# Converting float64 weights at two of every three second products instead of at each

## The chip, the cores and the metric

The kernel runs on one core of a Trainium2 chip. The metric is the device time of one execution in microseconds (us); of several executions the median counts. The core has five engines that each work through their own instruction list in order: TensorE (PE, with its weight loads shown apart as PEld), VectorE (DVE), ScalarE (ACT), GpSimd (POOL) and SyncE (SP), which here only issues transfers.

## The reference

Retention attention over 1152 tokens gives `x` (1152 x 512). Then comes a mixture of four experts, each `relu(x @ w1[e]) @ w2[e]`, weighted by probabilities and summed, and then one more block with other weights:

```python
def _moe2_ref(x, w_in, w_out):          # x (1152, 512), w_in (512, 2048), w_out (2048, 512)
    h = x @ w_in
    sp = np.where(h > 20.0, h, np.log1p(np.exp(np.minimum(h, 20.0))))
    g = h * np.tanh(sp)                 # mish
    return (g @ w_out).astype(np.float32)
```

`w_in` and `w_out` are float32 arrays multiplied by a float64 scalar and reach the kernel as float64, 8 bytes a value; the kernel makes float32r parts of them by taking their bits apart.

## The kernel before, in words

**Precision.** Every operand of a large matmul is held as two float32r parts, `hi` and `lo` (index 0 and 1 of a tile's second axis), and every product is three matmuls (hi·lo, hi·hi, lo·hi).

**Stages.** The attention stage fills the first 57 us or so. Then the two feed-forward blocks run as 144 *steps*, in the order that the list `seq` of `tile_order` gives; this text numbers them 0 to 143. A step is `("w1", u, c, tb)` or `("w2", u, c, tb)`: `u` is a slice of 512 hidden features (0 to 7 are the experts, 8 to 11 the last block), `c` one of two chunks of 256 output features, `tb` one of three blocks of 384 tokens. Each step is 24 matmuls of 128x128 weights by 128x384 into a tile `ps` of a PSUM pool with four buffers.

- A w1 step (`m1`; `first`, line 403) is followed by `relu_out`: ACT copies with Relu (L424), DVE takes the remainder (L425). From u = 8 on it is `mish_out`: ACT L433, ACT L434, DVE L435.
- A w2 step (`m2`; `second`, line 416) is followed on DVE by L463 (times the probabilities, out of PSUM) and L464 (add to `acc`); at u = 7 also by ACT L469 and POOL L470, which make the two parts of the next block's input `x2`. At u = 8 it is ACT L472, above that DVE L474.
- From step 6 to step 83 the list alternates w2 and w1 steps, in blocks of three token blocks: w2, w1, w2, w1, w2, w1. Such a run of six steps is called a *group* here. Steps 88 to 91 are four w2 steps in a row; step 92 is the first w1 step of the last block, and reads `x2` of token block 0; step 96 is the next that reads a new token block, `x2` of token block 1, which steps 91 and 93 make.

**Weights.** The experts' weights are float32: SP loads a chunk into a tile `wr` (L99), ACT makes `hi` (L114), POOL makes `lo` (L115). This is `split_w`, which runs once a chunk's buffer is free, in the alternating part twice a group, after the last two steps of the group.

**Float64 weights.** The last block has 16 chunks, each in two *halves*, 32 halves in all. One half goes through: a load by SP (L332, `load64`), `exponents64` (DVE L352, then ACT L356 and L357; DVE L358, L361), `values64` (DVE L371, L375, L378, then ACT L381, and the load of a later half), `rest64` (DVE L389), `store64` (SP L338, into a scratch tensor in device memory). From u = 8 on `split_w` only loads a finished chunk from that scratch tensor (L111). All these tiles and `wr` share one pool, `wraw`, of five buffers.

**What sets the order.** Everything is recorded under a manual schedule: each engine runs its instructions in the order in which the loop at the end of the kernel writes them. The loop takes up the four functions at every w2 step, `store64` and `values64` ahead of `m2`, `rest64` and `exponents64` behind it, so that one half is worked on by `exponents64` at one w2 step and by `values64` and `rest64` at the next. Such a w2 step is called a *turn* below. The 32 halves take the w2 steps 1 to 32 for `exponents64`, steps 6 to 68 of the list; the last store is written at step 72.

Of the kernel before, what the change touches and what calls it, by code (L numbers as in the profile page):

```python
# [59 lines left out]
def f32(ap):  # L60
    return ap.bitcast(F32)
# [3 lines left out]
def retention_moe_mish(ctx: ExitStack, tc: tile.TileContext, q2, k2, kt_in, v, vt_in, probs, w1, w2, w64, cdec, dec, out):  # L65
# [36 lines left out]
    def split_w(lo_engine):  # L102
        i = n_split[0]
        if i >= len(order):
            return
        n_split[0] += 1
        key = order[i]
        w = wsp.tile([P, 2, 4, 256], F32R, tag="w", name="w")
        w_t[key] = w
        if key[1] >= NE:  # L110
            sp.dma_start(out=f32(w), in_=scratch[key])  # L111
            return
        t = raw_t.pop(key)
        act.activation(out=w[:, 0], in_=t, func=AF.Copy)  # L114
        lo_engine.tensor_tensor(out=w[:, 1], in0=t, in1=f32(w[:, 0]), op=ALU.subtract)  # L115
        load_w()
# [207 lines left out]
    def load64():  # L324
        i = n_ld[0]
        if i >= len(halves):
            return
        n_ld[0] += 1
        (m, u, c), half = halves[i]
        t = wraw.tile([P, 2, 256, 2], U32, tag="wr", name="w64")  # L330
        src = w64[0 if m == "w1" else 1, u - NE, c, :, 2 * half:2 * half + 2]
        sp.dma_start(out=t, in_=src.bitcast(U32).rearrange("p k (n t) -> p k n t", t=2))  # L332
        raw64[i] = t

    def store64():
        if stores:
            key, half, t = stores.pop(0)
            sp.dma_start(out=scratch[key][:, :, 2 * half:2 * half + 2], in_=f32(t))  # L338
# [3 lines left out]
    def exponents64():  # L342

        i = n_cv[0]
        if i >= len(halves):
            return
        n_cv[0] += 1
        t = raw64.pop(i)
        lo_w, hi_w = t[:, :, :, 0], t[:, :, :, 1]
        g = ph.tile([P, 2, 256], F32, tag="g", name="g64", bufs=4)  # L350
        e = ph.tile([P, 2, 256], U32, tag="g", name="e64", bufs=4)
        dve.tensor_scalar(  # L352
            out=e, in0=hi_w, scalar1=20, scalar2=0x7FF,
            op0=ALU.logical_shift_right, op1=ALU.bitwise_and,
        )
        act.activation(out=e, in_=e, func=AF.Relu, bias=cbias[:, 0:1])  # L356
        act.activation(out=e, in_=e, func=AF.Relu, bias=cbias[:, 1:2], scale=-1.0)  # L357
        dve.tensor_scalar(  # L358
            out=g.bitcast(U32), in0=hi_w, scalar1=0xFFFFF, scalar2=None, op0=ALU.bitwise_and
        )  # L360
        dve.scalar_tensor_tensor(  # L361
            out=g, in0=lo_w, scalar=2.0 ** -32, in1=g.bitcast(U32), op0=ALU.mult, op1=ALU.add
        )
        flight.append((i, hi_w, g, e))

    def values64():
        if not flight or len(flight[0]) != 4:
            return
        i, hi_w, g, e = flight.pop(0)
        st = wraw.tile([P, 2, 2, 256], F32R, tag="wr", name="st64")  # L370
        dve.tensor_scalar(  # L371
            out=e, in0=e, scalar1=23, scalar2=0x7F800000,
            op0=ALU.logical_shift_left, op1=ALU.bitwise_xor,
        )
        dve.scalar_tensor_tensor(  # L375
            out=e, in0=hi_w, scalar=0x80000000, in1=e, op0=ALU.bitwise_and, op1=ALU.bitwise_or
        )
        dve.scalar_tensor_tensor(  # L378
            out=g, in0=g, scalar=2.0 ** 20, in1=e.bitcast(F32), op0=ALU.add, op1=ALU.mult
        )  # L380
        act.activation(out=st[:, 0], in_=g, func=AF.Copy, scale=2.0 ** -20)  # L381
        load64()
        flight.append((i, g, st))

    def rest64():
        if not flight or len(flight[0]) != 3:
            return
        i, g, st = flight.pop(0)
        dve.scalar_tensor_tensor(  # L389
            out=st[:, 1], in0=g, scalar=2.0 ** -20, in1=f32(st[:, 0]),  # L390
            op0=ALU.mult, op1=ALU.subtract,
        )
        stores.append((*halves[i], st))
# [47 lines left out]
    def m1(u, c, tb):  # L441
        o = first(x if u < NE else x2[0], w_t["w1", u, c], tb)
        h_t[u, c, tb] = relu_out(o) if u < NE else mish_out(o)

    def load_pb(e, tb):
        if e < E:
            pb = ph.tile([P, TB], F32, tag=f"pb{tb}", name="pb", bufs=1)
            row = p_dram[e:e + 1].rearrange("e n t -> e (n t)")[:, tb * TB:(tb + 1) * TB]
            sp.dma_start(out=pb, in_=row.to_broadcast([P, TB]))
            pb_t[e, tb] = pb  # L450

    def m2(u, c, tb, js=range(2)):
        ts = slice(tb * TB, (tb + 1) * TB)
        ks = slice(2 * c + js.start, 2 * c + js.stop)
        a = acc[:, ks, ts]
        o = second([h_t[u, i, tb] for i in range(2)], w_t["w2", u, c], js)
        if u < NE:
            pbb = pb_t[u // 2, tb].unsqueeze(1).to_broadcast([P, 2, TB])
            if u == 0:
                dve.tensor_tensor(out=a, in0=o, in1=pbb, op=ALU.mult)  # L460
                return
            t = ph.tile([P, 2, TB], F32, tag="n", name="t", bufs=3)
            dve.tensor_tensor(out=t, in0=o, in1=pbb, op=ALU.mult)  # L463
            dve.tensor_tensor(out=a, in0=a, in1=t, op=ALU.add)  # L464
            if u == NE - 1:
                if x2[0] is None:
                    x2[0] = keep.tile([P, 2, NPAIR, N], F32R, tag="x", name="x2")
                xo = x2[0][:, :, ks, ts]
                act.activation(out=xo[:, 0], in_=a, func=AF.Copy)  # L469
                pool.tensor_tensor(out=xo[:, 1], in0=a, in1=f32(xo[:, 0]), op=ALU.subtract)  # L470
        elif u == NE:
            act.activation(out=a, in_=o, func=AF.Copy)  # L472
        else:
            dve.tensor_tensor(out=a, in0=a, in1=o, op=ALU.add)  # L474
            if u == NU - 1:
                sp.dma_start(out=out[:, ks, ts], in_=a)

    with tc.manual_schedule():
        for tb in range(NTB):
            load_pb(0, tb)  # L480
        for i, (m, u, c, tb) in enumerate(seq):
            if m == "w1":
                m1(u, c, tb)
                if u == 0 and tb + 3 * c < 2:
                    load64()
            else:
                store64()
                values64()
                if i + 1 < len(seq):
                    m2(u, c, tb)  # L490
                else:
                    m2(u, c, tb, range(1))
                    m2(u, c, tb, range(1, 2))
                if u % 2 == 1 and c == 1:
                    load_pb(u // 2 + 1, tb)
                rest64()
                exponents64()
            k = n_split[0]
            if k < len(order) and last_use[order[k - 5]] <= i:
                split_w(pool)  # L500
# [67 lines left out]
```

## Time and profile before

| what | value |
|---|---|
| device time, median of 3 runs | 670.44 us (668.06 to 670.47) |
| the profiled execution | 667.62 us |
| its span on the core | 665.7 us |
| PE busy | 651.3 us, 98% of the span, 3846 matmuls |
| DVE busy | 355.1 us, 53% |
| ACT busy | 216.4 us, 32% |
| POOL busy | 98.1 us, 15% |
| granted TensorE clock, mean | 0.999 |

The span runs from the first to the last instruction; what lies around it is 667.62 − 665.70 = 1.92 us. Busy shares are means over the whole span: DVE's 53% is made of stretches over 80% and of stretches under 20%, so what DVE is worth must be read stretch by stretch. In the timeline a line is a run of instructions of one kind; behind it, in brackets, stands the time in which the engine did nothing before it, and what ended that.

### The profile page before, as it was taken

How to read it: one execution, taken by the hardware profiler on the slowest of the kernel's cores; microseconds unless marked ns; L12 is line 12 of the kernel's file. 1: busy time of each engine (PE TensorE's matmuls, PEld its weight loads, DVE VectorE, ACT ScalarE, POOL GpSimd, SP SyncE). 2: the span in 40 equal slices, each digit the busy share in tenths (PEclk: the TensorE clock that was granted, in tenths of full speed). 3: DMA queues.
4: the chain of work that ended last, by engine and by line, in shares of the span. 5: the costliest groups of instructions: out<-in, count | busy, mean ns of one | idle time of the engine just before them, and what ended most of it. 6: DMA issues, size and time to landing. Idle time of an engine off the chain costs nothing.

```text
span 665.7 us, 9178 instructions
## 1 busy us (share of the span) xinstructions
PE 651.3 (98%) x3846; PEld 646.9 (97%) x3846; DVE 355.1 (53%) x489; ACT 216.4 (32%) x296; POOL 98.1 (15%) x65
## 2 busy tenths in 40 slices
PE   7999999999999999999999999999999999999997
PEld 7999999999999999899898999999999999999997
DVE  4675267788787877888778733243311122222222
ACT  5773234434324344333443221112322211111200
POOL 4320202202022021120220331021100000000000
PEclk9999999999999999999999999999999999999999
DMA  8962224464654644545435311101312330330112
GB/s 295 391 233 82 82 79 142 147 203 128 194 159 130 194 133 145 187 162 193 138 118 189 119 44 51 63 15 48 127 65 77 115 138 1 111 142 1 64 48 95
DMA packets 30498, 83.99 MB, mean 126 GB/s; under 512 B 2994, under 2 KB 8698, under 8 KB 28410
## 3 DMA queue, kind: packets, MB, share of 16 engines
q1 hardware_dynamic: 30458, 83.42, 37.1%
q8 instruction: 30, 0.49, 0.3%
q14 instruction: 10, 0.08, 0.0%
HBM read 64.25 MB, written 19.15 MB: 125 GB/s over the span
## 4 chain that ended last, share of the span: by engine, by line
PE 63%; DVE 18%; ACT 7%; DMA 6%; issue 5%; SPq 1%; ACTq 0%
PE ps L403 28%; PE ps L416 28%; DVE e L375 5%; DMA w<-st 5%; DVE h L425 4%; ACT h L424 3%; PE ps L244 3%; DVE t L463 2%; DVE e L371 2%; ACT e L356 2%; PE ps L208 2%; DVE st L389 2%; ACT w L114 1%; DVE g L378 1%; DVE e L352 1%
## 5 line engine op out<-in xcount | busy, mean ns | idle before, releaser
L403 PE MATMUL ps<-x,w 128*128 128x384 f32 x1728 | 310.8, 335 | 3.4 <-DVE h L425 3.4
L416 PE MATMUL ps<-h,w 128*128 128x384 f32 x1728 | 310.3, 334 | 3.7 <-DVE t L463 3.7
L416 PEld LDWEIGHTS ps<-h,w 128*128 128x128 f32 x1728 | 300.2, 188 | 5.1 <-DVE t L463 5.0
L403 PEld LDWEIGHTS ps<-x,w 128*128 128x128 f32 x1728 | 300.1, 188 | 5.0 <-DVE h L425 5.0
L115 POOL TENSOR_TENSOR w<-wr,w 128x1024 fp32r<-128x1024 f32 x27 | 67.9, 2532 | 299.3 <-ACT w L114 265.3
L425 DVE SCALAR_TENSOR_TENSOR h<-ps,h 128x768 fp32r<-128x768 f32 x48 | 45.9, 957 | 89.8 <-ACT h L424 89.8
L435 DVE TENSOR_TENSOR h<-m,h 128x768 fp32r<-128x768 f32 x24 | 23.1, 960 | 126.2 <-ACT h L434 126.2
L424 ACT ACTIVATE h<-ps 128x768 fp32r<-128x768 f32 x48 | 38.4, 801 | 62.8 <-PE ps L403 57.6
L433 ACT ACTIVATE m<-ps 128x768 f32<-128x768 f32 x24 | 19.6, 815 | 113.5 <-PE ps L403 113.4
L381 ACT ACTIVATE st<-g 128x512 fp32r<-128x512 f32 x32 | 20.2, 633 | 111.2 <-DVE g L378 100.3
L463 DVE TENSOR_TENSOR t<-ps,pb 128x768 f32<-128x768 f32 x42 | 40.0, 952 | 26.7 <-PE ps L416 26.7
L356 ACT ACTIVATE e<-e,cbias 128x512 uint32<-128x512 uint32 x32 | 23.2, 725 | 65.7 <-DVE e L352 65.7
L375 DVE SCALAR_TENSOR_TENSOR e<-w,e 128x512 uint32<-128x512 uint32 x32 | 42.9, 1340 | 1.1
L464 DVE TENSOR_TENSOR acc<-acc,t 128x768 f32<-128x768 f32 x42 | 40.6, 966 | 1.4
L114 ACT ACTIVATE w<-wr 128x1024 fp32r<-128x1024 f32 x32 | 33.6, 1049 | 6.9 <-PE ps L416 6.8
L474 DVE TENSOR_TENSOR acc<-acc,ps 128x768 f32<-128x768 f32 (+1 forms) x19 | 17.3, 912 | 34.6 <-PE ps L416 34.6
L389 DVE SCALAR_TENSOR_TENSOR st<-g,st 128x512 fp32r<-128x512 f32 x32 | 24.1, 753 | 0.0
L357 ACT ACTIVATE e<-e,cbias 128x512 uint32<-128x512 uint32 x32 | 23.2, 724 | 1.0
L361 DVE SCALAR_TENSOR_TENSOR g<-w,g 128x512 f32<-128x512 uint32 x32 | 22.2, 693 | 1.1
L378 DVE SCALAR_TENSOR_TENSOR g<-g,e 128x512 f32<-128x512 f32 x32 | 22.1, 692 | 1.1
L371 DVE TENSOR_SCALAR e<-e 128x512 uint32<-128x512 uint32 x32 | 20.9, 652 | 0.0
L434 ACT ACTIVATE h<-m 128x768 fp32r<-128x768 f32 x24 | 20.4, 848 | 0.8
(46 smaller groups left out, 249.5 us busy)
## 6 DMA issues: line engine op xcount, KB each, us to landing
wr<-w SPq DMA_DIRECT2D x32, 512.0 KB, 4.0
w<-w SPq DMA_DIRECT2D x32, 512.0 KB, 3.9
w<-st SPq DMA_DIRECT2D x32, 512.0 KB, 4.8
w<-w SPq DMA_DIRECT2D x16, 1024.0 KB, 4.8
vr<-v SPq DMA_DIRECT2D x8, 288.0 KB, 5.4
pb<-p_dram SPq DMA_DIRECT2D x12, 192.0 KB, 3.7
kr<-k SPq DMA_DIRECT2D x7, 288.0 KB, 5.3
qr<-q SPq DMA_DIRECT2D x7, 288.0 KB, 6.4
```

Source lines behind the costliest of these rows:

```text
L114: act.activation(out=w[:, 0], in_=t, func=AF.Copy)
L115: lo_engine.tensor_tensor(out=w[:, 1], in0=t, in1=f32(w[:, 0]), op=ALU.subtract)
L356: act.activation(out=e, in_=e, func=AF.Relu, bias=cbias[:, 0:1])
L371: dve.tensor_scalar(out=e, in0=e, scalar1=23, scalar2=0x7F800000, op0=ALU.logical_shift_left, op1=ALU.bitwise_xor,)
L375: dve.scalar_tensor_tensor(out=e, in0=hi_w, scalar=0x80000000, in1=e, op0=ALU.bitwise_and, op1=ALU.bitwise_or)
L389: dve.scalar_tensor_tensor(out=st[:, 1], in0=g, scalar=2.0 ** -20, in1=f32(st[:, 0]), op0=ALU.mult, op1=ALU.subtract,)
L403: pe.matmul(o[:, j, :TB], w[:, a, k, fs], xs[:, c, k, ts], start=k == 0 and n == 0, stop=k == 3 and n == 2,)
L416: pe.matmul(o[:, j, :TB], w[:, a, f, ds_], h[:, c, f % 2], start=f == 0 and n == 0, stop=f == 3 and n == 2,)
L424: act.activation(out=h[:, 0], in_=o, func=AF.Relu)
L425: dve.scalar_tensor_tensor(out=h[:, 1], in0=o, scalar=0.0, in1=f32(h[:, 0]), op0=ALU.max, op1=ALU.subtract)
L463: dve.tensor_tensor(out=t, in0=o, in1=pbb, op=ALU.mult)
L464: dve.tensor_tensor(out=a, in0=a, in1=t, op=ALU.add)
```

## The change

The four conversion functions are no longer called at every w2 step, but only at two of three: a counter `n_y` counts the w2 steps, and where it is a multiple of three the step is written without them. Nothing else differs; the operations, their shapes and their number are the same. In the alternating part the third w2 step of each group, `tb` = 2, is without a turn. The 32 halves now take w2 steps 1 to 47 for `exponents64`: the last is step 97 of the list, and the last store comes at step 102.

```diff
+        n_y = 0
         for i, (m, u, c, tb) in enumerate(seq):
...
             else:
-                store64()
-                values64()
+
+                n_y += 1
+                turn = n_y % 3 != 0
+                if turn:
+                    store64()
+                    values64()
                 if i + 1 < len(seq):
                     m2(u, c, tb)
...
-                rest64()
-                exponents64()
+                if turn:
+                    rest64()
+                    exponents64()
```

Two places show how instructions move. The first is DVE's list in the alternating part (the experts with u = 5). Before, every pair of a w1 and a w2 step reads like this one; `e`, `g`, `w` and `st` are the tiles of a half, `h`, `t` and `acc` those of the steps:

```order
L425 SCALAR_TENSOR_TENSOR h<-ps,h 128x768
L371 TENSOR_SCALAR e_2053<-e_2053 128x512
L375 SCALAR_TENSOR_TENSOR e_2053<-w_1949,e_2053 128x512
L378 SCALAR_TENSOR_TENSOR g_2052<-g_2052,e_2053 128x512
L463 TENSOR_TENSOR t<-ps,pb 128x768
L464 TENSOR_TENSOR acc<-acc,t 128x2x384
L389 SCALAR_TENSOR_TENSOR st_2088<-g_2052,st_2088 128x512
L352 TENSOR_SCALAR e_2125<-w_2021 128x512
L358 TENSOR_SCALAR g_2124<-w_2021 128x512
L361 SCALAR_TENSOR_TENSOR g_2124<-w_2021,g_2124 128x512
```

With the change two pairs of three read as above, and the third is bare; here is the end of a turn, the bare pair and the beginning of the next turn:

```order
L352 TENSOR_SCALAR e_2397<-w_2289 128x512
L358 TENSOR_SCALAR g_2396<-w_2289 128x512
L361 SCALAR_TENSOR_TENSOR g_2396<-w_2289,g_2396 128x512
L425 SCALAR_TENSOR_TENSOR h<-ps,h 128x768
L463 TENSOR_TENSOR t<-ps,pb 128x768
L464 TENSOR_TENSOR acc<-acc,t 128x2x384
L425 SCALAR_TENSOR_TENSOR h<-ps,h 128x768
L371 TENSOR_SCALAR e_2397<-e_2397 128x512
L375 SCALAR_TENSOR_TENSOR e_2397<-w_2289,e_2397 128x512
L378 SCALAR_TENSOR_TENSOR g_2396<-g_2396,e_2397 128x512
```

What moved: the bare pair has three DVE instructions instead of ten, and what followed stands later in the list.

The second place is DVE's list around steps 88 to 93, where the experts end and the last block begins. Before, no conversion is left there; from step 88 on the list reads:

```order
L463 TENSOR_TENSOR t<-ps,pb 128x768
L464 TENSOR_TENSOR acc<-acc,t 128x2x384
L463 TENSOR_TENSOR t<-ps,pb 128x768
L464 TENSOR_TENSOR acc<-acc,t 128x2x384
L463 TENSOR_TENSOR t<-ps,pb 128x768
L464 TENSOR_TENSOR acc<-acc,t 128x2x384
L463 TENSOR_TENSOR t<-ps,pb 128x768
L464 TENSOR_TENSOR acc<-acc,t 128x2x384
L435 TENSOR_TENSOR h<-m,h 128x768
```

With the change turns stand at steps 88, 90 and 91. From the L463 of step 90 on:

```order
L463 TENSOR_TENSOR t<-ps,pb 128x768
L464 TENSOR_TENSOR acc<-acc,t 128x2x384
L389 SCALAR_TENSOR_TENSOR st_3756<-g_3718,st_3756 128x512
L352 TENSOR_SCALAR e_3793<-w_3684 128x512
L358 TENSOR_SCALAR g_3792<-w_3684 128x512
L361 SCALAR_TENSOR_TENSOR g_3792<-w_3684,g_3792 128x512
L371 TENSOR_SCALAR e_3793<-e_3793 128x512
L375 SCALAR_TENSOR_TENSOR e_3793<-w_3684,e_3793 128x512
L378 SCALAR_TENSOR_TENSOR g_3792<-g_3792,e_3793 128x512
L463 TENSOR_TENSOR t<-ps,pb 128x768
L464 TENSOR_TENSOR acc<-acc,t 128x2x384
```

What moved: two consecutive w2 steps (90 and 91) now have a whole half's work between their products.

## Rows read from the trace of the kernel before

**Rows 1.** Part 1 of the page, TensorE: busy time, share of the span, instructions.

```profile
PE 651.3 (98%) x3846; PEld 646.9 (97%) x3846; DVE 355.1 (53%) x489; ACT 216.4 (32%) x296; POOL 98.1 (15%) x65
```

**Rows 2.** Busy time by stretch: length, then each engine, granted clock, DMA share, GB/s.

```profile
250.00:300.00 50.00, 47.45 (x271) 46.49 (x270) 41.42 (x55) 18.32 (x25) 9.90 (x4) 1.00 0.50 166
...
450.00:500.00 50.00, 50.00 (x290) 50.00 (x289) 13.42 (x14) 14.16 (x18) 6.08 (x4) 1.00 0.24 85
```

**Rows 3.** Who TensorE waited for: us in total, times, longest us.

```profile
PE ps L416 <- DVE t L463: 3.7, 4, 0.9
PE ps L403 <- DVE h L425: 3.4, 5, 0.7
```

**Rows 4.** Timeline of TensorE: steps 7, 47, 88 to 91, and 92.

```profile
82.21 4.32 PE L403 MATMUL ps<-x,w 128*128 128x384 f32 x24
...
249.58 4.43 PE L403 MATMUL ps<-x,w 128*128 128x384 f32 x24 [0.68 <-DVE h L425]
...
428.99 16.80 PE L416 MATMUL ps<-h,w 128*128 128x384 f32 x96
...
445.63 4.32 PE L403 MATMUL ps<-x,w 128*128 128x384 f32 x24
```

**Rows 5.** Timeline of DVE: one ordinary pair, from its L371 to the next.

```profile
249.45 0.41 DVE L371 TENSOR_SCALAR e<-e 128x512 uint32<-128x512 uint32 x1
...
251.23 0.95 DVE L463 TENSOR_TENSOR t<-ps,pb 128x768 f32<-128x768 f32 x1
...
252.22 0.96 DVE L464 TENSOR_TENSOR acc<-acc,t 128x768 f32<-128x768 f32 x1
...
253.09 0.69 DVE L389 SCALAR_TENSOR_TENSOR st<-g,st 128x512 fp32r<-128x512 f32 x1
...
256.36 0.96 DVE L425 SCALAR_TENSOR_TENSOR h<-ps,h 128x768 fp32r<-128x768 f32 x1 [1.18 <-ACT h L424]
257.24 0.42 DVE L371 TENSOR_SCALAR e<-e 128x512 uint32<-128x512 uint32 x1
```

**Rows 6.** Timeline of POOL and DVE: the pair in which POOL splits weights.

```profile
264.45 4.95 POOL L115 TENSOR_TENSOR w<-wr,w 128x1024 fp32r<-128x1024 f32 x2 [22.20 <-ACT w L114]
...
265.98 1.16 DVE L371 TENSOR_SCALAR e<-e 128x512 uint32<-128x512 uint32 x1
...
267.17 2.77 DVE L375 SCALAR_TENSOR_TENSOR e<-w,e 128x512 uint32<-128x512 uint32 x1
...
293.12 1.16 DVE L371 TENSOR_SCALAR e<-e 128x512 uint32<-128x512 uint32 x1
```

**Rows 7.** Timeline after the conversion: a bare pair's L463 and L464 beside POOL.

```profile
383.43 0.96 DVE L463 TENSOR_TENSOR t<-ps,pb 128x768 f32<-128x768 f32 x1 [2.36 <-PE ps L416]
...
384.42 0.96 DVE L464 TENSOR_TENSOR acc<-acc,t 128x768 f32<-128x768 f32 x1
384.62 3.02 POOL L115 TENSOR_TENSOR w<-wr,w 128x1024 fp32r<-128x1024 f32 x1 [10.01 <-ACT w L114]
```

**Rows 8.** DMA issues: KB each, median us from issue to landing (half loaded, half stored).

```profile
w<-w SPq DMA_DIRECT2D x32, 512.0 KB, 3.9
w<-st SPq DMA_DIRECT2D x32, 512.0 KB, 4.8
```

**Rows 9.** Timeline of the hand-over: L463 of step 88, table load, x2 of step 93, step 96.

```profile
433.35 0.96 DVE L463 TENSOR_TENSOR t<-ps,pb 128x768 f32<-128x768 f32 x1 [2.35 <-PE ps L416]
...
448.68 1.28 ACT L433 ACT_TABLE_LOAD   x1
...
457.06 1.84 POOL L470 TENSOR_TENSOR x<-acc,x 128x768 fp32r<-128x768 f32 x1 [6.48 <-ACT x L469]
...
462.27 4.32 PE L403 MATMUL ps<-x,w 128*128 128x384 f32 x24
```

**Rows 10.** Groups of instructions on ACT: busy us, mean ns of one, idle before.

```profile
L433 ACT ACTIVATE m<-ps 128x768 f32<-128x768 f32 x24 | 19.6, 815 | 113.5 <-PE ps L403 113.4
...
L356 ACT ACTIVATE e<-e,cbias 128x512 uint32<-128x512 uint32 x32 | 23.2, 725 | 65.7 <-DVE e L352 65.7
```

## The prediction

> **What bounds the kernel now.** The page's first part comes first: TensorE is busy for 98% of the span [rows 1], so only what stops TensorE, or runs before or after it, can be worth anything. Then the busy times by stretch: in 450 to 500 us TensorE is busy all the time and DVE for 13.42 us of 50; in 250 to 300 us TensorE lacks 2.55 us and DVE is busy for 41.42 us [rows 2]. The granted clock is 1.00 in both, so the clock explains nothing. The waits name the engine: TensorE waits nine times for DVE, 3.7 + 3.4 = 7.1 us in all [rows 3], each time for a PSUM buffer that DVE has not read out.
>
> These 7.1 us are not the whole loss, since a stalled step's matmuls are also drawn longer (4.43 us for a step instead of 4.32). The starts tell it better. Steps 88 to 92 start 445.63 − 428.99 = 16.64 us apart over four steps, 4.16 us a step. From step 7 (82.21) to step 88 (428.99) are 81 steps, which at 4.16 would be 336.96 us; they took 346.78 [rows 4]. **The conversion stretch loses 9.82 us.**
>
> Why DVE is late there: an ordinary pair of steps costs it 257.24 − 249.45 = 7.79 us [rows 5], under TensorE's 2 × 4.16 = 8.32. But once a group POOL splits two chunks, and then L371 takes 1.16 us instead of 0.42 and L375 2.77, while the pair of POOL operations lasts [rows 5, 6]. So a group costs DVE 293.12 − 265.98 = 27.14 us [rows 6], against 6 × 4.16 = 24.96 for TensorE. DVE loses 2.18 us a group. For the first groups the four PSUM buffers hide that; the first stall is at step 47 [rows 4].
>
> **The change, part by part.**
>
> *The group.* One pair of three loses its conversion. Of 7.79 us the bare pair keeps L463 until L464 starts (252.22 − 251.23 = 0.99), L464 (253.09 − 252.22 = 0.87) and L425 (257.24 − 256.36 = 0.88), 2.74 in all; 1.18 is idle time before L425, behind ACT's two conversion operations [rows 5]. What is surely gone is 7.79 − 2.74 − 1.18 = 3.87 us. The group becomes at most 27.14 − 3.87 = 23.27 us, 1.69 below TensorE's 24.96. DVE then waits for TensorE once a group and starts each group without a debt; within a group the split pair of 27.14 − 2 × 7.79 = 11.56 us is 3.24 above 8.32, and three other PSUM buffers (12.5 us of TensorE's work) stand between it and a stall. I take the whole 9.82 us. The value is bounded below by what a collision in the bare pair could take back (second rival).
>
> *POOL and ACT.* Without conversion operations ahead of it, ACT makes the first `hi` right at the end of the skipped step, so POOL's first split now runs beside the bare pair. A bare pair beside POOL exists in this trace: L464 at 384.42 takes 0.96 us, and POOL, which starts 0.20 later, takes 3.02 [rows 7]. There POOL waits and DVE does not. So I cost this at nothing; at worst L464 waits for one POOL operation, 4.95 / 2 = 2.47 us [rows 6].
>
> *SP.* The number of transfers is the same. In its list a turn's store now stands behind the two weight loads of the group, and the load that follows waits for that store's buffer. Counted from the end of the skipped step: the second split can start after the next w1 step (4.16) and ACT's work, about 6.2, and ends by 8.7; then the store lands after 4.8 and the load after 3.9 [rows 8], at 17.4. DVE wants that half at the second turn, whose w2 step ends at 4 × 4.16 = 16.64, behind L463, L464 and L389, at about 19.3. Margin 1.9 us: nothing, and a miss would move only DVE, which has 1.69 us a group to spare.
>
> *The hand-over to the last block.* The turns that are left over now stand in steps 78 to 102. The point that matters is step 96, which needs `x2` of step 93. Before, POOL has it at 457.06 + 1.84 = 458.90, 3.37 us ahead of step 96 at 462.27 [rows 9]. Worked out from the end of step 88, which is 0; L463 follows it by 0.2. Three costs of a turn from rows 5: L463 and L464 1.86; L389 to L361 about 2.0; L371 to L378 1.78 (251.23 − 249.45). Steps 89, 90, 91 end at 4.16, 8.32, 12.48. DVE: step 88's products until 2.1, its half until 4.1; step 89's products 4.4 to 6.2; `values64` until 8.0; step 90's products 8.5 to 10.4, its half until 12.4; then `values64` waits for ACT's two operations (0.73 each [rows 10]) until 13.0 and ends at 14.8; step 91's products until 16.6. Its L352 starts at 17.2, and from here the chain goes over ACT: 0.46 to L356, L356 and L357 1.5, the table load 1.28 [rows 9], L433 0.82 [rows 10] and L434, taken as long, 0.82, which gives 22.1; L435, taken like L464, 0.9, step 93's products 1.95, L469, taken like L433, 0.85, POOL 1.84 [rows 9]: **27.6**. Step 96 starts seven steps after the end of step 88, at 7 × 4.16 = 29.12, and needs this half of `x2` only with its seventh matmul, at 30.16. So no stall, by 2.5 us. But POOL's 1.84 us run beside this work, and each time that DVE must wait for one, as in rows 6, the chain is 1.84 later: two of them give 31.3 (a stall of 1.1), three 33.1 (3.0). I take 0.5 us, between none and one and a half; the ends are 0 and 3.0.
>
> No row shows L470 beside a conversion. The Trainium skill, in "SBUF — State Buffer", section "SBUF: two separate sides", says that the port pair shared by VectorE and GpSimd is an exclusive lock, held for a whole instruction by whichever starts first. By it L470 collides as L115 does in rows 6 and 7, and speaks against this change at the hand-over only: the span would take the upper end of this term, 3.0 us more than without a collision; rows 6 and 7 agree with the rule, but show that either side may be the one that waits.
>
> *The sum.* The span is 665.70 − 9.82 + 0.5 = 656.4 us; with the 1.92 around it 658.3. The profiled execution (667.62) lies 2.82 under the median of the runs shown (670.44), two of which agree within 0.03, so I set the forecast against the median: **661.1 us**, 1.4% less.
>
> **The rivals.**
>
> *Half of it comes back.* The hand-over stalls at step 96 and again at step 103, where token block 2 arrives, or loads come late in some groups: 1 to 6 us. For it: the chain above has ten links, with 2.5 us to spare. Against it: step 103 has three more steps of margin. Time about 664.5, up to 667.
>
> *DVE stays the bound: no change.* The place is the bare pair. If L464 waited 2.47 us in every group, a group would be 25.74, 0.78 above TensorE; over 13 groups that is 10.1 us, most of which the PSUM buffers and the slack of the first groups absorb, as they did before: there nine groups of 2.18 are 19.6 us, and 9.82 were lost. To lose the whole gain a group must reach about 24.96 + (9.8 + 9.8) / 13 = 26.5, 3.2 us more than worked out, more than one POOL operation. Time 668 to 671.
>
> *Slower: the hand-over becomes a new bound.* From step 85 on eight turns stand where there were none: about 7 × 3.87 = 27 us of DVE work, and 6 × 1.84 of POOL beside it. If `x2` or PSUM put all of it on TensorE's path, the time were 661 + 27 = 688. It decides when more than 9.8 + 3.4 = 13.2 us of it, half, reaches TensorE. Against it: DVE is busy for 13.42 us of 50 there [rows 2], and TensorE waits for DVE only by PSUM, four buffers deep, and by `x2`.
>
> *The change does less than it says.* A finished half might be needed earlier than it is stored. The lists exclude it: the closest pair is the last, stored at step 102 and read from step 133 on.
>
> **How the numbers follow.** What a measurement of this kernel can tell from no change is about 0.5%, 3.4 us. Forecast 0.75; half comes back 0.15; no change 0.07; slower 0.03. Faster by over 0.5% (under 667.1) are the first two, 0.90; the same 0.07; slower 0.03. The range reaches from the full 9.82 off the profiled execution, less 0.8, a third of the 2.4 us between the runs shown (667.62 − 9.82 − 0.8 = 657.0), to the middle of the second case and somewhat above, 665.5. The forecast's own range is 657.8 to 663.5.
>
> **What would show it.** Right: no wait of TensorE for DVE L425 or L463 in 200 to 400 us; step 88 at about 82.2 + 81 × 4.16 = 419.2; a bare pair in each group with DVE idle before L463; POOL's pairs 24.96 us apart instead of 27.14; at most one TensorE wait for POOL L470. Wrong: waits of TensorE for DVE that go on at lower counts (second rival), or gaps in TensorE between steps 92 and 104 of more than 3 us in all (first and third).

## The result and the profile after

The changed kernel takes 659.86 us, the median of four runs (658.09 to 662.28), against 670.02 for the kernel before (four runs, 668.06 to 670.47). The ratio is 0.9856 with a 95% interval of 0.9818 to 0.9894: **1.4% faster**, clear of the 0.5% that can be told from no change. The forecast was 661.1, range 657.0 to 665.5. The profiled execution took 660.29 us, with a span of 658.4.

The first part of the page answers to [rows 1]:

```profile
PE 650.0 (99%) x3846; PEld 648.3 (98%) x3846; DVE 357.2 (54%) x489; ACT 217.7 (33%) x296; POOL 104.1 (16%) x65
```

No engine lost work. TensorE is busy for 1.3 us less, and DVE and POOL are busier, by 2 and 6 us, since an operation that waits for the other engine is drawn longer (POOL's L115 3.02 us instead of 2.40 in the rows further down). The gain stands only in the waits. These are all the waits of TensorE in the changed kernel (engine, line and what was waited for; us in total, times, longest):

```profile
PE ps L225 <- POOL qg L188: 2.3, 1, 2.3
PE ps L281 <- DVE zero L267: 1.2, 1, 1.2
PE ps L244 <- ACT v L201: 1.1, 1, 1.1
PE ps L208 <- ACT k L178: 0.2, 1, 0.2
```

All four lie in the first 12 us. The two rows of [rows 3], nine waits for DVE, are gone. The busy times by stretch (columns as in [rows 2]) show where the conversion went:

```profile
250.00:300.00 50.00, 50.00 (x290) 50.00 (x289) 35.77 (x46) 16.77 (x22) 11.14 (x4) 1.00 0.44 138
...
450.00:500.00 50.00, 50.00 (x290) 49.85 (x289) 27.06 (x33) 19.28 (x26) 5.71 (x3) 1.00 0.39 132
```

DVE is busy for 35.77 us of 50 in the alternating part instead of 41.42, and for 27.06 instead of 13.42 where the last block begins; TensorE lacks nothing in either. In the timeline of TensorE (the first number is the start in us, the second the duration), steps 7, 88 to 91, 92, 96 and 97, to be held against [rows 4]:

```profile
84.56 4.32 PE L403 MATMUL ps<-x,w 128*128 128x384 f32 x24
...
421.52 16.80 PE L416 MATMUL ps<-h,w 128*128 128x384 f32 x96
438.16 4.32 PE L403 MATMUL ps<-x,w 128*128 128x384 f32 x24
...
454.80 4.45 PE L403 MATMUL ps<-x,w 128*128 128x384 f32 x24
459.08 4.32 PE L416 MATMUL ps<-h,w 128*128 128x384 f32 x24
```

From step 7 to step 88 it takes 421.52 − 84.56 = 336.96 us, which is 81 × 4.16 to the hundredth, where it took 346.78. Step 96 takes 459.08 − 454.80 = 4.28, 0.12 more than a step.

One thing runs against the gain. Step 6 starts at 80.40 us in this profile and at 78.05 in the profile of before, though the attention stage ahead of it is the same in both. Counted from step 6 to the end the spans are 658.4 − 80.40 = 578.0 and 665.7 − 78.05 = 587.65: 9.65 us less, not the 7.3 that the two spans show.

Here is one bare pair and the turn behind it, on DVE, ACT and POOL:

```profile
201.24 0.96 DVE L463 TENSOR_TENSOR t<-ps,pb 128x768 f32<-128x768 f32 x1 [1.34 <-PE ps L416]
201.28 1.06 ACT L114 ACTIVATE w<-wr 128x1024 fp32r<-128x1024 f32 x1 [2.38 <-issue]
202.23 0.96 DVE L464 TENSOR_TENSOR acc<-acc,t 128x768 f32<-128x768 f32 x1
202.42 3.02 POOL L115 TENSOR_TENSOR w<-wr,w 128x1024 fp32r<-128x1024 f32 x1 [17.60 <-ACT w L114]
...
206.24 0.96 DVE L425 SCALAR_TENSOR_TENSOR h<-ps,h 128x768 fp32r<-128x768 f32 x1 [3.06 <-ACT h L424]
207.12 0.42 DVE L371 TENSOR_SCALAR e<-e 128x512 uint32<-128x512 uint32 x1
207.23 2.55 POOL L115 TENSOR_TENSOR w<-wr,w 128x1024 fp32r<-128x1024 f32 x1 [1.79 <-ACT w L114]
207.57 2.76 DVE L375 SCALAR_TENSOR_TENSOR e<-w,e 128x512 uint32<-128x512 uint32 x1
...
227.38 3.02 POOL L115 TENSOR_TENSOR w<-wr,w 128x1024 fp32r<-128x1024 f32 x1 [17.60 <-ACT w L114]
```

What to see: DVE waits 1.34 us for TensorE before L463 (before, the wait was the other way round), and 3.06 us before L425, for ACT's L424 behind the next w1 step. L464 starts 0.19 us ahead of POOL, keeps its 0.96, and POOL takes 3.02, as in [rows 7]. L375 still waits for POOL's second operation, 2.76 us as in [rows 6]; that costs nothing any more, since the group has room for it. POOL's first operations stand 227.38 − 202.42 = 24.96 us apart, TensorE's pace.

### The profile page after: what moved, and what is told of

The parts are those of the page before. It is cut to its first block, busy times and chain, and to the rows that moved or that the text cites. A ratio compares the mean times of both kernels' runs of the same rounds, so it can differ in the third digit from the quotient of the medians.

```text
span 658.4 us, 9160 instructions
## 1 busy us (share of the span) xinstructions
PE 650.0 (99%) x3846; PEld 648.3 (98%) x3846; DVE 357.2 (54%) x489; ACT 217.7 (33%) x296; POOL 104.1 (16%) x65
## 4 chain that ended last, share of the span: by engine, by line
PE 98%; DMA 1%; SPq 1%; ACT 0%; DVE 0%; issue 0%
PE ps L403 46%; PE ps L416 45%; PE ps L244 3%; PE ps L208 2%; PE ps L254 1%; DMA vr<-v 1%; PE ps L225 1%; ACT v L201 0%; SPq L156 0%; SPq L155 0%; DVE acc L474 0%; SPq L165 0%; SPq L164 0%; SPq L163 0%; SPq L161 0%
## 5 line engine op out<-in xcount | busy, mean ns | idle before, releaser
L115 POOL TENSOR_TENSOR w<-wr,w 128x1024 fp32r<-128x1024 f32 x27 | 73.4, 2718 | 284.0 <-ACT w L114 251.7
L425 DVE SCALAR_TENSOR_TENSOR h<-ps,h 128x768 fp32r<-128x768 f32 x48 | 45.9, 957 | 99.5 <-ACT h L424 99.5
L424 ACT ACTIVATE h<-ps 128x768 fp32r<-128x768 f32 x48 | 38.6, 804 | 68.0 <-PE ps L403 62.9
L463 DVE TENSOR_TENSOR t<-ps,pb 128x768 f32<-128x768 f32 x42 | 40.0, 952 | 15.9 <-PE ps L416 15.9
L375 DVE SCALAR_TENSOR_TENSOR e<-w,e 128x512 uint32<-128x512 uint32 x32 | 47.0, 1469 | 1.1
L114 ACT ACTIVATE w<-wr 128x1024 fp32r<-128x1024 f32 x32 | 33.9, 1058 | 32.9 <-issue 21.4
L464 DVE TENSOR_TENSOR acc<-acc,t 128x768 f32<-128x768 f32 x42 | 40.2, 958 | 1.4
L361 DVE SCALAR_TENSOR_TENSOR g<-w,g 128x512 f32<-128x512 uint32 x32 | 26.8, 836 | 1.1
L378 DVE SCALAR_TENSOR_TENSOR g<-g,e 128x512 f32<-128x512 f32 x32 | 25.2, 789 | 1.1
L389 DVE SCALAR_TENSOR_TENSOR st<-g,st 128x512 fp32r<-128x512 f32 x32 | 21.9, 683 | 0.7 <-ACT st L381 0.7
L470 POOL TENSOR_TENSOR x<-acc,x 128x768 fp32r<-128x768 f32 x6 | 11.6, 1932 | 61.9 <-ACT x L469 61.9
L244 PE MATMUL ps<-ret,v 128*128 128x128 f32 (+2 forms) x144 | 19.8, 296 | 1.1 <-ACT v L201 1.1
```

What stands on the lines that cost most here:

```text
L244: pe.matmul(o[:, c * D:c * D + w], vv[:, c].rearrange("p j d -> p (j d)"), ret[:, t, off:off + w], start=c in (0, 6), stop=False,)
L361: dve.scalar_tensor_tensor(out=g, in0=lo_w, scalar=2.0 ** -32, in1=g.bitcast(U32), op0=ALU.mult, op1=ALU.add)
L375: dve.scalar_tensor_tensor(out=e, in0=hi_w, scalar=0x80000000, in1=e, op0=ALU.bitwise_and, op1=ALU.bitwise_or)
L378: dve.scalar_tensor_tensor(out=g, in0=g, scalar=2.0 ** 20, in1=e.bitcast(F32), op0=ALU.add, op1=ALU.mult)
L424: act.activation(out=h[:, 0], in_=o, func=AF.Relu)
L425: dve.scalar_tensor_tensor(out=h[:, 1], in0=o, scalar=0.0, in1=f32(h[:, 0]), op0=ALU.max, op1=ALU.subtract)
```

## The experiments

Steps are compared by their starts, which the trace gives to a hundredth of a microsecond; "lost in the loop" is the start of step 88 less that of step 6 less 82 × 4.16 = 341.12, and "lost in step 96" is the time from step 96 to step 97 less 4.16.

| kernel | step 6 | step 88 | lost in the loop | lost in step 96 | step 6 to the end |
|---|---|---|---|---|---|
| before | 78.05 | 428.99 | 9.82 | 0 | 587.65 |
| changed | 80.40 | 421.52 | 0 | 0.12 | 578.0 |
| changed, again | 78.22 | 419.33 | 0 | 0.12 | 578.0 |
| before, low parts on DVE | 78.00 | 419.12 | 0 | 0.01 | 577.8 |
| five turns of six | 79.51 | 420.63 | 0 | 0 | 577.8 |
| bare pair filled | 78.52 | 432.30 | 12.66 | 3.74 | 594.4 |
| bare pair first | 80.07 | 421.19 | 0 | 1.43 | 579.2 |
| turn at step 89 too | 78.41 | 419.53 | 0 | 6.51 | 584.4 |

### The changed kernel once more

No edit. It asks whether the later start of step 6 belongs to the change.

> The changed kernel once more. Theory (DVE's list was longer than TensorE's per group of six steps, the bare pair makes it shorter): from step 6 to step 95 every step starts 4.16 us after the one before, step 96 loses 0 to 0.3 us, and the span from step 6 to the end is 578.0 us as in the first profile. The 2.35 us by which step 6 started later in the first profile of the change (80.40 against 78.05) lie in the attention stage, which the change does not touch: theory, they are scatter, and step 6 starts anywhere from 77.5 to 80.5. Rival: the change delays the attention stage, and step 6 starts at 80.4 again, within 0.2.

Measured: 660.12 us against 669.06, ratio 0.9852 (0.9816 to 0.9888); step 6 at 78.22, span 656.2, the steps as before. So the 2.35 us are scatter of the attention stage, and the rival falls. What goes with the scatter can be seen in the stretch from 10 to 15 us (columns as in [rows 2]), first of the changed kernel, then of the same kernel in this run:

```profile
10.00:15.00 5.00, 3.88 (x19) 3.88 (x20) 1.12 (x4) 4.58 (x9) 2.05 (x3) 0.66 1.05 388
```

```profile
10.00:15.00 5.00, 4.42 (x37) 4.42 (x38) 1.12 (x4) 4.78 (x9) 2.06 (x3) 1.00 1.05 391
```

The granted clock is 0.66 there in the one and 1.00 in the other. The group of matmuls at L244 has 18 instructions in both timelines:

```profile
11.12 3.96 PE L244 MATMUL ps<-ret,v 128*128 128x128 f32 x18 [1.13 <-ACT v L201]
```

```profile
10.58 2.32 PE L244 MATMUL ps<-ret,v 128*128 128x128 f32 x18 [1.17 <-ACT v L201]
```

They take 3.96 us at the lower clock and 2.32 at the higher. Before that TensorE had waited 2.3 us at L225 in the first and 1.3 in the second. Of the eight profiles of this study three show 0.66 in that stretch (the changed kernel, five turns of six, bare pair first), and these are the three in which step 6 starts after 79 us. They are also the three with the longest wait at L225, 1.7 to 2.3 us against 1.2 to 1.5 in the other five. Whether that wait lowers the clock, and what lengthens it, was not tried.

### The low parts made by DVE, in the kernel before

```diff
-                split_w(pool)
+                split_w(dve)
```

The turns stand at every w2 step, as before; POOL has nothing left to do beside the conversion.

> The kernel before, a turn at every second product, but the low parts of the experts' weights are made by DVE instead of POOL, so POOL has no operation beside the conversion. Theory (the split pair's 11.56 us against 7.79 are DVE waiting while POOL holds a port): a group costs DVE 27.14 - 3.77 + 2 x 1.23 = 25.8 us, 0.9 over TensorE; over nine groups 7.8 us, which the slack of the first groups (9 x 2.18 - 9.82 = 9.8 us before) absorbs, so 0 to 1.5 us are lost and the kernel is 8 to 10 us faster than before. Rival (the 3.77 us come from ACT's order, with its two weight copies ahead of L424, and not from the port): a group costs 27.14 + 2.45 = 29.6, and the kernel is some 20 us slower than before.

Measured: 660.2 us, ratio 0.9852 (0.9817 to 0.9888), no loss in the loop. A stretch of DVE's timeline, from the split pair of one group to that of the next:

```profile
310.51 1.22 DVE L115 TENSOR_TENSOR w<-wr,w 128x1024 fp32r<-128x1024 f32 x1 [1.43 <-ACT w L114]
311.65 0.95 DVE L425 SCALAR_TENSOR_TENSOR h<-ps,h 128x768 fp32r<-128x768 f32 x1
312.52 1.21 DVE L115 TENSOR_TENSOR w<-wr,w 128x1024 fp32r<-128x1024 f32 x1
313.65 0.42 DVE L371 TENSOR_SCALAR e<-e 128x512 uint32<-128x512 uint32 x1
314.10 0.69 DVE L375 SCALAR_TENSOR_TENSOR e<-w,e 128x512 uint32<-128x512 uint32 x1
...
339.56 0.42 DVE L371 TENSOR_SCALAR e<-e 128x512 uint32<-128x512 uint32 x1
```

The group is 339.56 − 313.65 = 25.91 us, against 25.8 expected: DVE took over POOL's work and its list became 1.23 us shorter all the same than the 27.14 of [rows 6]. L375 takes 0.69 everywhere, so the waiting for POOL is gone, and this one word gains as much as the change.

The 3.77 us of the expectation were not all waiting for POOL, though. In the kernel before, L371 and L375 of the split pair are longer by 0.74 + 2.08 = 2.82 us [rows 5, 6]. The other 0.95 is idle time before its L425, 2.13 us instead of the 1.18 of [rows 5], because ACT makes a weight copy (L114) ahead of L424:

```profile
263.33 1.04 ACT L114 ACTIVATE w<-wr 128x1024 fp32r<-128x1024 f32 x1
264.27 0.80 ACT L424 ACTIVATE h<-ps 128x768 fp32r<-128x768 f32 x1
265.10 0.96 DVE L425 SCALAR_TENSOR_TENSOR h<-ps,h 128x768 fp32r<-128x768 f32 x1 [2.13 <-ACT h L424]
```

With the low parts on DVE, 1.43 us of that idle time are left, and the two L115 cost 1.14 + 1.13 from their starts to the next. So 2.8 us of each group before were DVE waiting for POOL, and the rival is right about the 0.95.

In this kernel DVE is still slower than TensorE, by 25.91 − 24.96 = 0.95 us a group: nine groups lose 8.6 us, and all of it is absorbed by slack. What counts is a debt and how much of it fits into the slack, not whether DVE is the slower engine.

### The bare pair filled

Five operations are added that compute nothing of use (`acc` times `acc` into a spare tile):

```diff
                 if turn:
                     rest64()
                     exponents64()
+                elif n_y < 40:
+                    fill = ph.tile([P, 2, TB], F32, tag="n", name="fill", bufs=3)
+                    a = acc[:, 2 * c:2 * c + 2, tb * TB:(tb + 1) * TB]
+                    for _ in range(5):
+                        dve.tensor_tensor(out=fill, in0=a, in1=a, op=ALU.mult)
```

> The changed kernel, with five more DVE operations (acc times acc into an unused tile, 128x768, some 0.96 us each, 4.5 to 4.9 us) behind L464 in each bare pair of the first 39 second products; no ACT operation, no transfer is added. Theory (what counts is the length of DVE's list): a group costs DVE 22.1 to 23.3 + 4.7 = 26.8 to 28.0 us, POOL's first splits stand that far apart, TensorE waits for DVE again, and of 13 x 1.8 to 3.0 us about 9.8 are absorbed: 14 to 30 us slower than the changed kernel. Rival (the change helped by spreading the transfers and the weight buffers, or by taking ACT's two operations out of the way of L424): no wait of TensorE for DVE, within 1 us of the changed kernel.

Measured: 674.69 us in one run, span 672.9, against 669.06 for the kernel before and 660.12 for the changed one. TensorE waits for DVE again (waits of this kernel):

```profile
PE ps L403 <- DVE h L425: 10.5, 7, 1.5
PE ps L403 <- POOL x L470: 2.0, 1, 2.0
```

```profile
258.10 5.48 POOL L115 TENSOR_TENSOR w<-wr,w 128x1024 fp32r<-128x1024 f32 x2 [21.27 <-ACT w L114]
284.85 5.48 POOL L115 TENSOR_TENSOR w<-wr,w 128x1024 fp32r<-128x1024 f32 x2 [21.27 <-ACT w L114]
```

```profile
258.96 2.35 DVE L464 TENSOR_TENSOR acc<-acc,t 128x768 f32<-128x768 f32 x1
261.35 7.02 DVE L508 TENSOR_TENSOR fill<-acc 128x768 f32<-128x768 f32 x5
```

Here L508 is the added operation; the five take 7.02 us and not 4.5 to 4.9, because one of them waits for POOL's second operation. POOL's operations stand 26.75 us apart (expected 26.8 to 28.0); the loop loses 12.66 us and step 96 another 3.74, together 16.4 (expected 14 to 30). The transfers and ACT's order are those of the changed kernel, so they are not what the change gained by: the length of DVE's list is. L464 also shows the second rival's mechanism. Where DVE is late, POOL starts first (258.10 against 258.96) and L464 takes 2.35 us. Reckoned as 13 groups of 26.75 − 24.96 = 1.79 us, the debt is 23.3 us, of which the slack took 23.3 − 12.66 = 10.6; before, by the same reckoning, it took 9 × 2.18 − 9.82 = 9.8.

### Five turns of six

```diff
-                turn = n_y % 3 != 0
+                turn = n_y % 6 != 0
```

> Turns at five of six second products instead of two of three. Theory (only the mean length of DVE's list over the groups counts, as long as the slack of the first groups lasts): two groups cost DVE 27.14 + 22.1 to 23.3 = 49.2 to 50.4 us against 49.92 of TensorE; no stall in the loop, 0 to 0.5 us; conversion over by step 88, so x2 for step 96 is ready 3 us or more ahead instead of just in time. Same time as the changed kernel within 0.5 us of its steps. Rival (each group needs its own bare pair): the groups without one stall as before, about 2 us each, 6 us in all.

Measured: 659.84 us, ratio 0.9848 (0.9807 to 0.989), no loss in the loop: every second group may be as long as before. And the hand-over is free again; these are the rows of POOL's `x2` of step 93 and of step 96:

```profile
448.70 1.84 POOL L470 TENSOR_TENSOR x<-acc,x 128x768 fp32r<-128x768 f32 x1 [6.48 <-ACT x L469]
```

```profile
453.91 4.32 PE L403 MATMUL ps<-x,w 128*128 128x384 f32 x24
```

`x2` is ready at 448.70 + 1.84 = 450.54, 3.37 us ahead of step 96, as in [rows 9]. The time is the changed kernel's and the margin is over 3 us, both as expected.

### The bare pair first

```diff
-                turn = n_y % 3 != 0
+                turn = n_y % 3 != 1
```

> Turns at two of three second products, but the bare pair is the first of a group (token block 0), the one in which L375 met POOL's second split, instead of the last. Theory (length of DVE's list per group; which pair is bare only moves the collision): no wait of TensorE for DVE in the loop, steps 6 to 91 at 4.16 us. The turns near the end now stand at steps 88, 89, 91 and 93, and x2 for step 96 comes at 29.7 to 31.3 us after the end of step 88 against 30.16: 0 to 1.1 us of stall there. Rival (it is the last pair that must be bare, because only there the split pair's surplus is paid back before the next group): waits of TensorE for DVE in the loop, 1 us a group or more.

Measured: 661.22 us in one run, no loss in the loop, so which pair is bare does not matter there, and the rival falls. The collision did move: L375 takes 0.69 us everywhere, and now L464 of the bare pair waits for POOL's second split, which starts at 208.70:

```profile
210.22 1.70 DVE L464 TENSOR_TENSOR acc<-acc,t 128x768 f32<-128x768 f32 x1
```

Step 96 waits for POOL:

```profile
456.82 3.40 PE L403 MATMUL ps<-x,w 128*128 128x384 f32 x18 [1.15 <-POOL x L470]
```

`x2` came at 454.77 + 1.99 = 456.76, 31.4 us after the end of step 88 (421.19 + 4.16), against 31.3 at the upper end of what was worked out; step 96 loses 1.43 us, a little more than the 0 to 1.1 expected.

### A turn at step 89 too

```diff
-                turn = n_y % 3 != 0
+                turn = n_y % 3 != 0 or n_y == 42
```

> The changed kernel with one more turn, at step 89, so that the four second products 88 to 91 all have one; the loop before is the same. Theory (the hand-over has no margin left: DVE's list between step 88 and step 93 and ACT's chain behind it set when step 96 can go on): x2 of step 93 comes 32.7 to 34.2 us after the end of step 88, a wait of TensorE for POOL L470 in step 96 of 2.5 to 4.1 us and no wait elsewhere over 0.5 us. Rival (four PSUM buffers and TensorE's lead hide the hand-over as they hide the loop): no wait over 0.3 us.

Measured: 664.75 us in one run. The wait is the expected one, 3.53 us, and the only one of the main part; but step 96 loses 6.51 us. POOL's `x2` and the two pieces of step 96 in the timeline, then the stretches around it:

```profile
452.81 1.21 PE L403 MATMUL ps<-x,w 128*128 128x384 f32 x6
455.69 1.80 POOL L470 TENSOR_TENSOR x<-acc,x 128x768 fp32r<-128x768 f32 x1 [6.29 <-ACT x L469]
457.55 6.13 PE L403 MATMUL ps<-x,w 128*128 128x384 f32 x18 [3.53 <-POOL x L470]
463.48 4.37 PE L416 MATMUL ps<-h,w 128*128 128x384 f32 x24
```

```profile
450.00:456.00 6.00, 4.01 (x24) 3.69 (x22) 2.78 (x3) 3.08 (x5) 0.31 (x1) 1.00 0.27 98
456.00:464.00 8.00, 6.45 (x21) 6.45 (x22) 6.61 (x10) 2.82 (x5) 1.49 (x1) 0.57 0.16 68
464.00:470.00 6.00, 6.00 (x37) 6.00 (x36) 3.88 (x6) 2.59 (x4) 0.00 (x0) 1.00 0.34 116
```

`x2` is ready 455.69 + 1.80 − 423.69 = 33.8 us after the end of step 88 (419.53 + 4.16 = 423.69), as expected. Then the eighteen matmuls behind the wait take 463.48 − 457.55 = 5.93 us to the start of the next step instead of 3.12 (18 × 4.16 / 24): the mean granted clock is 0.57 from 456 to 464 us. So the slow matmuls cost 2.81 us on top of the wait. The theory holds, and the rival falls. The size of the wait was expected; the cost of the lower clock behind it was not.

## Why the prediction was right

**What bounds the kernel** held: the loss was 9.82 us of stalls on DVE, and all of it went. The first profile, the repeat and three other edits that shorten DVE's list (low parts on DVE, five turns of six, the bare pair first) each give 0 in the loop; the edit that lengthens it brings the loss back.

**The group** held: DVE's list fell under TensorE's, and DVE waits for TensorE in each bare pair, 1.34 us before L463 and, by way of ACT's L424, before L425. That the length of this list is the cause is shown by the filled bare pair; that 2.8 us of it were waiting for POOL, by the low parts on DVE. The prediction named only L371 and L375 as the reason of the 27.14 us; 0.95 of them were the later L425. Its sum went by the whole group, so it did not suffer.

**POOL and ACT** held: L464 keeps 0.96, POOL pays 3.02. The prediction's bound for L464, 2.47 us of waiting, is within reach: where POOL starts first, L464 takes 2.35 us (filled bare pair) or 1.70 (bare pair first).

**SP** held: no wait of DVE for a load appears, and steps keep their pace.

**The hand-over** was the term with the loosest size: taken at 0.5 us, a value between two cases, and measured at 0.12. That the two lie so close is in part luck, since collisions used up the 2.5 us that the chain had to spare. The chain was worked out to come at 27.6 us after the end of step 88 without a collision and 31.3 with two. Its rows in the changed kernel:

```profile
429.13 2.22 DVE L361 SCALAR_TENSOR_TENSOR g<-w,g 128x512 f32<-128x512 uint32 x1
...
434.31 2.25 DVE L378 SCALAR_TENSOR_TENSOR g<-g,e 128x512 f32<-128x512 f32 x1
...
445.96 2.22 DVE L361 SCALAR_TENSOR_TENSOR g<-w,g 128x512 f32<-128x512 uint32 x1
...
447.13 1.28 ACT L433 ACT_TABLE_LOAD   x1
...
453.92 1.85 POOL L470 TENSOR_TENSOR x<-acc,x 128x768 fp32r<-128x768 f32 x1 [6.29 <-ACT x L469]
```

Step 88 ends at 421.52 + 4.16 = 425.68, and `x2` is there at 453.92 + 1.85 = 455.77: 30.09 us later, where 30.16 was needed. There were three collisions, in which L361 and L378 take 2.22 and 2.25 us instead of their usual 0.69: 1.53 to 1.56 us each and not 1.84. The third ran beside ACT's part of the chain, so two counted. These rows agree with the lock rule that the prediction drew from the Trainium skill ("SBUF — State Buffer", section "SBUF: two separate sides"), L470 meeting the conversion as L115 does. The 3.0 us that the prediction put beside the rule did not come, since only two collisions counted.

**The rivals.** "Half comes back" did not happen, but only just: `x2` came 0.07 us ahead of its need, and one more turn at step 89, or turns at 89 and 93 instead of 90, cost 6.51 and 1.43 us there. "No change" had its mechanism right, but it needs POOL to start ahead of L464. In the changed kernel L464 starts 0.19 us ahead of POOL, and the mechanism does not set in. "Slower" fell; it needed 13.2 us of conversion work to reach TensorE and 0.12 did; even the denser hand-over lost 6.51.

**The sum.** From step 6 on it gave 665.7 − 78.05 − 9.82 + 0.5 = 578.3 us, measured 578.0. The span came out at 658.4 instead of 656.4 because the attention stage took 2.35 us more in that execution, which no term held; in the repeat the span is 656.2. The range allowed for the scatter of the runs, and covered it.

## What to carry to other kernels

A helper engine that is 53% busy over the span can still stall the main one: compare the length of its list in one period with the period of the main engine, waits included, and count the debt over the periods against the slack that the buffers give. Spreading such work was free here until it reached a place where one chain of several engines must meet a deadline; look there first for what the spreading costs, and prefer the spreading that ends ahead of it (five turns of six gives the same time here, with `x2` ready 3.4 us ahead of step 96). An operation of DVE that waits for POOL is drawn as busy (L375 2.77 us instead of 0.69), so compare the longest duration of an operation with its usual one.

## What the runs showed of the hardware

A wait of TensorE can cost about twice its length. After 3.53 us of waiting in step 96 (turn at step 89 too) this stretch stands at 0.50, the lower level of 1.2 GHz:

```profile
458.00:460.00 2.00, 2.00 (x8) 2.00 (x8) 1.93 (x4) 0.00 (x0) 0.00 (x0) 0.50 0.00 0
```

The step lost 6.51 us. After 2.02 us (filled bare pair) it lost 3.74, and the clock was lower there too:

```profile
470.00:472.00 2.00, 2.00 (x9) 2.00 (x8) 1.97 (x3) 0.61 (x1) 0.00 (x0) 0.59 0.01 4
```

After waits of 1.49 to 1.52 us (seven times in the filled bare pair), of 1.15 (bare pair first) and of 0.68 to 0.94 (before) the clock stayed at 1.00. In the first 15 us a lower clock goes with 1.64 of the 80.40 − 78.22 = 2.18 us between the two profiles of the changed kernel: 3.96 us for 18 matmuls at L244, or 2.32. The other 0.54 lie ahead of it, since L244 starts at 11.12 us in the one and at 10.58 in the other.
